# A replanned first phase: seven heads begun on half of D, 2 KB weight rows, K transposed by TensorE, LN statistics split over two engines, all pinned in order

## The chip, the cores and the metric

The kernel runs on one core of a Trainium2 chip. The metric is device time of one execution in microseconds (us), lower is better. All runs named here are of the state "fast"; one core has no second die to compare with.

## The reference

One transformer block with conditioning: a modulation vector from `c`, a layer norm (LN), attention with 32 heads over a cached window of 512 keys in four K/V groups, a second LN, and a SwiGLU block. All arrays are bf16; S = 2048, D = 1024.

```python
mod = (silu(c) @ w_mod).reshape(1, 6, 1, -1)       # sa, ca, ga, sb, cb, gb
h = layernorm(x) * (1 + ca) + sa
q = (h @ wq)                                        # 32 heads of 128
p = softmax(q @ k[last 512].T * 128 ** -0.5)        # k, v from the cache
x = x + ga * ((p @ v) @ wo)
h = layernorm(x) * (1 + cb) + sb
x = x + gb * ((silu(h @ w_gate) * (h @ w_up)) @ w_down)
```

## The kernel before

The sequence is cut into four chunks of 512 rows. After a first phase, which loads x, the columns of `w_mod` and the first weights and makes h of chunk 0, a loop of 128 steps (chunk and head) does attention; the SwiGLU stage follows. In step k TensorE (PE) does the scores of head k, q of a head LEAD steps ahead, side tasks of that step, and the output of head k-1. `at(k, f, ...)` puts a task in step k. All loads and the transposing DMAs go through one queue, that of SyncE (SP). `pin` keeps an instruction in program order on its engine; it is switched off after the loop, and a scheduler orders what isn't pinned.

```python
    for half in range(DH):                 # DMA order of the first phase
        load_wm(1, half)                   # w_mod columns of ca, 1 MB, rows of 1 KB
        load_wm(0, half)                   # of sa
        load_wq(0, 0, (half,))             # wq of heads 0-3, half of D, 0.5 MB
    ...                                    # kT by transposing DMA, then v
    LEAD = 3
    for t in range(QT):                    # LN of chunk 0: four tiles, statistics on DVE
        ln_stats(t)
        n = ln_norm(t, t % 2 == 0)         # tiles 0 and 2 normalised by ACT
        for dt in range(DT):
            nc.tensor.transpose(h0_ps[dt // 4][:, dt % 4, t * P:(t + 1) * P], ...)
        warm(2)                            # dummy matmuls
    for half in range(DH):
        mod_cols(1, half, ca1, True)       # 32 narrow matmuls
        mod_cols(0, half, sa, False)
        ...                                # affine of four dt, then q of heads 0-2 on this half
    # [...]
    at(16 * n + 16, load_cols, n, 2, ..., n == 0)   # small DMA, then 1 + on DVE in the same step
    # [...]
    def plan_late_ln(k, key, sc, sh):      # second LN of the last chunk, in the SwiGLU stage
        for t in range(QT):
            at(k + 2 * t, late_stats, tt)
            at(k + 10 + 2 * t, ln_rows, tt)        # normalise (DVE)
            at(k + 11 + 2 * t, ln_xpose, key, tt)  # transposing DMA
    # [...]
    for k in range(NU + 1):
        if k % 4 >= 2 and 4 * (k // 4) + 8 < NU:
            g = 4 * (k // 4) + 8
            load_wq(g // H, (g % H) // 4, (k % 4 - 2,))   # one half of a wq group
        emit_s(k); emit_q(k + LEAD); run_tasks(k); emit_o(k - 1)   # shortened
    stage.update(dma=False, steps=False)   # from here on nothing is pinned
```

Of the kernel before, what the change touches and what calls it, by code (L numbers as in the profile page):

```python
# [9 lines left out]
ALU = mybir.AluOpType  # L10
# [578 lines left out]
def fast_path(ctx, tc, flag, A_x, A_k_cache, A_v_cache, A_wq, A_wo, B_x, B_w_gate, B_w_up,  # L589
# [36 lines left out]
    k_v = A_k_cache[0][:, k0:k0 + W, :].rearrange("kv (j p) d -> p kv j d", p=P)  # L626
    v_v = A_v_cache[0][:, k0:k0 + W, :].rearrange("kv (j p) d -> p kv j d", p=P)
# [6 lines left out]
    pc_ = ctx.enter_context(tc.tile_pool(name="blkC", bufs=12))  # L634
# [34 lines left out]

    nc.scalar.preload_act_table_set("natural_log_exp_and_others")  # L670
# [23 lines left out]

    for tt in range(QT):
        load_x(tt)
    for half in range(DH):
        load_wm(1, half)
        load_wm(0, half)
        load_wq(0, 0, (half,))  # L700
    kT = blkB("kT", [P, Hkv, W])
    for kv in range(Hkv):
        pin(nc.sync.dma_start_transpose(
            out=kT[:, kv, :], in_=A_k_cache[0, kv, k0:k0 + W, :]), "dma")
# [4 lines left out]
    nc.gpsimd.memset(v_sb[:, :, :, Dh:VN], 1.0)  # L709
    load_wq(0, 1)  # L710


    ident = const.tile([P, P], BF16, name="ident")
    make_identity(nc, ident)
    ones_bf = const.tile([P, P], BF16, name="ones_bf")
# [3 lines left out]

    warm_w = const.tile([P, 512], BF16, name="warm_w")  # L720
    nc.gpsimd.memset(warm_w, 0.5)
    warm_ps = mm("warm_ps")

    def warm(n):
        for _ in range(n):
            tc.keep_in_program_order(
                nc.tensor.matmul(warm_ps, lhsT=ones_bf, rhs=warm_w, start=True, stop=True))

    warm(16)
# [5 lines left out]

    ec = wk.tile([DT, P], FP32, name="ec", tag="f32", bufs=2)
    nc.scalar.activation(out=ec, in_=c_r, func=ACT.Exp, scale=-1.0)
    nc.vector.tensor_scalar(out=ec, in0=ec, scalar1=1.0, scalar2=None, op0=ALU.add)
    rc = wk.tile([DT, P], FP32, name="rc", tag="f32", bufs=2)
    nc.vector.reciprocal(out=rc, in_=ec)  # L740
    sil_r = const.tile([DT, P], BF16, name="sil_r")
    nc.vector.tensor_tensor(out=sil_r, in0=c_r, in1=rc, op=ALU.mult)
    sil_ps = mm("sil_ps", (P, DT), BF16)
    nc.tensor.transpose(sil_ps, sil_r, ident[0:DT, 0:DT])
    siluc = const.tile([P, DT], BF16, name="siluc")
    nc.vector.tensor_copy(out=siluc, in_=sil_ps)
# [11 lines left out]



    sil32 = const.tile([P, DT, 32], BF16, name="sil32")
    for dt in range(DT):
        nc.vector.tensor_scalar(out=sil32[:, dt, :], in0=ones_bf[:, 0:32],
                                scalar1=siluc[:, dt:dt + 1], scalar2=None, op0=ALU.mult)
# [123 lines left out]
    def plan_late_ln(k, key, sc, sh):  # L888

        for t in range(QT):  # L890
            tt = key[1] * QT + t
            at(k + 2 * t, late_stats, tt)
            at(k + 10 + 2 * t, ln_rows, tt)
            at(k + 11 + 2 * t, ln_xpose, key, tt)
        at(k + 8, late_rstd)
        for dt in range(DT):
            at(k + 24 + dt, ln_mod, key, dt, sc, sh)
# [13 lines left out]
    LEAD = 3  # L911
    qT = {}

    def put_q(g, q_ps):
        t = wk.tile([P, TCW], BF16, name="qT", tag="row", bufs=5)
        nc.vector.tensor_copy(out=t, in_=q_ps)  # L916
        qT[g] = t



    new_hT(("h1", 0))
    h0_ps = [big("h0_ps", (P, 4, TCW), BF16) for _ in range(2)]
    for t in range(QT):
        ln_stats(t)
        n = ln_norm(t, t % 2 == 0)
# [3 lines left out]
        warm(2)  # L929
    q0_ps = []  # L930
    for half in range(DH):
        mod_cols(1, half, ca1, True)
        mod_cols(0, half, sa, False)
        for dt in range(4 * half, 4 * half + 4):
            ln_affine(("h1", 0), dt, h0_ps[half][:, dt % 4, :], ca1, sa, dt % 2 == 0)
        if half == 0:
            q0_ps = [mm("q_ps") for _ in range(LEAD)]
        for n in range(4 * LEAD):
            dt, g = (4 * half + n // LEAD, n % LEAD) if half == 0 else (4 + n % 4, n // 4)
            nc.tensor.matmul(q0_ps[g],  # L940
                             lhsT=wq_tiles[(0, 0, dt // 4)][:, dt % 4, g * P:(g + 1) * P],
# [332 lines left out]
```

## Time and profile before

| | before |
|---|---|
| time, median of 4 runs (range) | 1285.27 us (1284.90 to 1288.04) |
| PE busy, share of the span | 1269.7 us, 99% |
| first scores (s_ps) start | 26.46 us |
| PE's longer gaps after that | 0.9 us at 91 us, 2.3 us at 752 us |

The page's head and its first engine line:

```profile
span 1282.7 us, 18139 instructions
...
PE 1269.7 (99%) x7601; PEld 642.9 (50%) x7601; DVE 577.8 (45%) x1271; ACT 333.9 (26%) x433; POOL 1.2 (0%) x8
...
```

PE is the limit everywhere but in the first 30 us. The list of waits from 32 us to the end gives the total, the count and the longest wait in us. A gap quoted in the text runs from the start of one matmul to the start of the next, less their usual spacing (0.216 us for 512 columns); the views count from a modelled end, which makes the same gap about 0.16 us shorter (2.3 us in the table, 2.1 here):

```profile
PE gu_ps L1168 <- DMA wu<-in_B_w_up_dram: 2.1, 1, 2.1
...
PE a_ps L1096 <- DVE acc L1102: 0.7, 1, 0.7
...
```

So what a change can gain lies almost all in the first phase. Its time line (start, duration, engine, instruction, shapes, count; in brackets the idle time before it and what ended it):

```profile
15.62 1.06 PE L927 MATMUL h_ps<-ident,xn 128*128 128x128 bf16 x8
...
17.32 1.51 PE L940 MATMUL q_ps<-hT,wq 128*128 128x512 bf16 x6
...
21.25 0.95 PE L753 MATMUL mod_ps<-siluc,wm 128*128 128x1 bf16 x32 [0.35 <-DMA wm<-in_w_mod_dram]
...
26.46 1.02 PE L1032 MATMUL s_ps<-qT,kT 128*128 128x512 bf16 x4
...
```

The fourth tile's transposes start at 15.6 us, q of the first three heads on the first half of D at 17.3, the last `mod_cols` at 21.25 once the last `wm` has landed, and the scores at 26.46. The windows below give the stretch, its length, the busy us of PE, PEld, DVE, ACT and POOL (instructions in brackets), granted PE clock, DMA share and GB/s:

```profile
12.00:14.00 2.00, 0.85 (x33) 0.86 (x34) 0.00 (x0) 1.38 (x3) 0.00 (x0) 1.00 1.10 348
14.00:16.00 2.00, 2.00 (x18) 1.44 (x16) 0.63 (x2) 0.00 (x0) 0.00 (x0) 0.50 1.10 347
16.00:18.00 2.00, 2.00 (x12) 1.10 (x10) 0.54 (x1) 1.10 (x2) 0.00 (x0) 0.65 1.10 351
...
```

The DMA engines are full at about 350 GB/s, while PE works at a granted clock of 0.50 from 14 to 17.4 us after a thin stretch.

### The profile page before, as it was taken

Reading aid. Unit: us, or ns where it says so; the run is one execution under the profiler, and the core shown is the slowest. Engines: PE = TensorE matmul, PEld = TensorE weight load, DVE = VectorE, ACT = ScalarE, POOL = GpSimd, SP = SyncE. Lnnn points to the kernel's source line nnn. Section 1 sums busy time; section 2 is a strip of 40 time slices with the busy share of each in tenths; the row PEclk is TensorE's granted clock in tenths of the full one; section 3 lists DMA queues with packets and bytes.
Section 4 is the critical chain, followed back from the end, with each engine's and each line's share of the span. In section 5 each row is a group of like instructions: output and inputs, shape, how many; then the busy total and the mean of one; then the engine's idle time right before and its main releaser. Section 6 shows DMA issues by size and latency. Waiting matters only on the chain.

```text
span 1282.7 us, 18139 instructions
## 1 busy us (share of the span) xinstructions
PE 1269.7 (99%) x7601; PEld 642.9 (50%) x7601; DVE 577.8 (45%) x1271; ACT 333.9 (26%) x433; POOL 1.2 (0%) x8
## 2 busy tenths in 40 slices
PE   8999999999999999999999999999999999999998
PEld 4555555555555555555554444444444444444444
DVE  4464467865577755576653642221212221221122
ACT  3543334333333433333341111011100111011100
POOL 0000000000000000000000000000000000000000
PEclk9999999999999999999999999999999999999999
DMA  9888476557355654445487484454536455454401
GB/s 293 269 204 232 152 154 167 141 149 195 91 129 155 144 148 140 123 142 131 132 207 221 142 234 150 140 189 147 181 102 216 143 165 164 135 193 134 146 21 48
DMA packets 280108, 204.21 MB, mean 159 GB/s; under 512 B 113865, under 2 KB 273609, under 8 KB 280018
## 3 DMA queue, kind: packets, MB, share of 16 engines
q1 hardware_dynamic: 275106, 198.78, 54.2%
q10 hardware_dynamic: 4912, 4.20, 1.0%
q8 instruction: 61, 1.00, 0.3%
q14 instruction: 29, 0.24, 0.1%
HBM read 174.08 MB, written 4.21 MB: 139 GB/s over the span
## 4 chain that ended last, share of the span: by engine, by line
PE 95%; DMA 2%; DVE 1%; SPq 1%; ACT 0%; issue 0%; DVEq 0%
PE gu_ps L1168 29%; PE a_ps L1096 17%; PE q_ps L1019 17%; PE d_ps L1188 15%; PE o_ps L1064 9%; PE s_ps L1032 8%; DMA wm<-in_w_mod_dram 1%; SPq L664 1%; DMA hT<-xn 0%; DMA modT<-row_d 0%; DMA wu<-in_B_w_up_dram 0%; PE row_ps L779 0%; PE q_ps L940 0%; DVE st L816 0%; SPq L848 0%; ACT pT L1034 0%
## 5 line engine op out<-in xcount | busy, mean ns | idle before, releaser
L1034 ACT ACTIVATE pT<-s_ps 128x1024 bf16<-128x1024 f32 x256 | 248.7, 1020 | 341.8 <-PE s_ps L1032 341.8
L1096 PE MATMUL a_ps<-wo,oT 128*128 128x512 bf16 x1024 | 241.9, 379 | 0.7 <-DVE acc L1102 0.7
L1019 PE MATMUL q_ps<-hT,wq 128*128 128x512 bf16 x1000 | 236.7, 379 | 0.3 <-DVE modT L755 0.3
L1168 PE MATMUL gu_ps<-hT,wu 128*128 128x512 bf16 x896 | 211.8, 379 | 2.1 <-DMA wu<-in_B_w_up_dram 2.1
L1168 PE MATMUL gu_ps<-hT,wg 128*128 128x512 bf16 x896 | 211.7, 379 | 0.0
L1174 DVE TENSOR_TENSOR guT<-gu_ps,sg 128x512 bf16<-128x512 f32 x112 | 77.4, 691 | 283.5 <-ACT sg L1173 283.5
L1173 ACT ACTIVATE sg<-gu_ps 128x512 bf16<-128x512 f32 x112 | 66.9, 597 | 490.9 <-PE gu_ps L1168 439.7
L1188 PE MATMUL d_ps<-wd,guT 128*128 128x512 bf16 (+2 forms) x952 | 194.2, 366 | 0.0
L916 DVE CAST qT<-q_ps 128x512 bf16<-128x512 f32 x128 | 88.3, 691 | 176.6 <-PE q_ps L1019 176.0
L1096 PEld LDWEIGHTS <-oT 128*128 128x128 bf16 x1024 | 99.9, 98 | 122.1 <-issue 1.9
L1019 PEld LDWEIGHTS <-wq 128*128 128x128 bf16 x1000 | 97.8, 98 | 117.8 <-issue 0.3
L1188 PEld LDWEIGHTS <-guT 128*128 128x128 bf16 x952 | 90.9, 98 | 102.9
L1064 PEld LDWEIGHTS <-pT 128*128 128x128 bf16 x2048 | 126.6, 98 | 30.6 <-issue 0.4
L1168 PEld LDWEIGHTS <-wu 128*128 128x128 bf16 x896 | 87.6, 98 | 108.1 <-DMA wu<-in_B_w_up_dram 2.6
L1168 PEld LDWEIGHTS <-wg 128*128 128x128 bf16 x896 | 87.7, 98 | 105.4
L1064 PE MATMUL o_ps<-v_sb,pT 128*128 128x130 bf16 x2048 | 137.1, 220 | 0.0
L1032 PE MATMUL s_ps<-qT,kT 128*128 128x512 bf16 x512 | 131.5, 379 | 0.6 <-ACT pT L1034 0.6
L1051 DVE TENSOR_TENSOR oq<-o_ps,rl 128x256 bf16<-128x256 f32 (+2 forms) x256 | 101.3, 420 | 4.3
L1192 DVE TENSOR_TENSOR f<-d_ps,gb_bc 128x512 f32<-128x512 f32 (+2 forms) x34 | 22.5, 661 | 147.0 <-PE d_ps L1188 147.0
L1104 DVE TENSOR_TENSOR acc<-a_ps,acc 128x512 f32<-128x512 f32 x64 | 44.1, 689 | 38.9 <-PE a_ps L1096 38.9
L1032 PEld LDWEIGHTS <-kT 128*128 128x128 bf16 x512 | 44.9, 98 | 31.7 <-issue 1.3
L816 DVE BATCH_NORM_STATS2 st<-x 128x6 f32<-128x512 bf16 x64 | 41.3, 680 | 2.9 <-DMA x<-in_A_x_dram 2.6
(75 smaller groups left out, 309.3 us busy)
## 6 DMA issues: line engine op xcount, KB each, us to landing
wq<-in_A_wq_dram SPq DMA_DIRECT2D x64, 512.0 KB, 4.1
wo<-in_A_wo_dram SPq DMA_DIRECT2D x64, 512.0 KB, 5.5
wg<-in_B_w_gate_dram SPq DMA_DIRECT2D x56, 512.0 KB, 5.1
wu<-in_B_w_up_dram SPq DMA_DIRECT2D x56, 512.0 KB, 3.8
wd<-in_B_w_down_dram SPq DMA_DIRECT2D x56, 512.0 KB, 6.4
wmr<-in_w_mod_dram SPq DMA_DIRECT2D x8, 1024.0 KB, 11.4
x<-in_A_x_dram SPq DMA_DIRECT2D x16, 256.0 KB, 5.7
wm<-in_w_mod_dram SPq DMA_DIRECT2D x4, 1024.0 KB, 10.5
```

The costliest lines, as they stand in the source:

```text
L916: nc.vector.tensor_copy(out=t, in_=q_ps)
L1019: nc.tensor.matmul(q_ps, lhsT=wq_tiles[(cc, h // 4, dt // 4)][:, dt % 4, (h % 4) * P:(h % 4 + 1) * P], rhs=hT[("h1", cc)][:, dt, :], start ...
L1032: nc.tensor.matmul(s_ps[:, i, :], lhsT=kT[:, kv, j * P:(j + 1) * P], rhs=qT[g], start=True, stop=True)
L1034: nc.scalar.activation(out=p[:, 2 * jj:2 * jj + 2, :], in_=s_ps, func=ACT.Exp, scale=scale)
L1051: nc.vector.tensor_tensor(out=dst, in0=ps[:, s0:s0 + cnt, 0:Dh], in1=sc, op=ALU.mult)
L1064: nc.tensor.matmul(o_slot["ps"][:, s_, :], lhsT=pT[g][:, j, t * P:(t + 1) * P], rhs=v_sb[:, kv, j, 0:VN], start=(j == 0), stop=(j == WT - 1))
L1096: nc.tensor.matmul(a_ps, lhsT=oT[(cc, 2 * q + i)][:, hh % 4, t * P:(t + 1) * P], rhs=wo_tiles[(cc, q, dh, i)][:, hh % 4, :], start=(hh == ...
L1104: nc.vector.tensor_tensor(out=acc[(cc, t)][:, dsl], in0=a_ps, in1=acc[(cc, t)][:, dsl], op=ALU.add)
L1168: nc.tensor.matmul(ps[:, n, :], lhsT=gu_w[(cc, fg, nm, dt // 4)][:, dt % 4, fi * P:(fi + 1) * P], rhs=hT[("h2", cc)][:, dt, :], start=(dt ...
L1173: nc.scalar.activation(out=g, in_=ps[:, 0, :], func=ACT.Silu)
L1174: nc.vector.tensor_tensor(out=guT[(cc, fg)][:, fi, :], in0=ps[:, 1, :], in1=g, op=ALU.mult)
L1188: nc.tensor.matmul(d_ps, lhsT=guT[(cc, f // 4)][:, f % 4, t * P:(t + 1) * P], rhs=wd_tiles[(cc, dh, f // 4)][:, f % 4, c0:c0 + w], start=( ...
```

## The change

The intent: the phase waits for 5.8 MB (four x tiles of 256 KB, four `wm` of 1024 KB, one wq of 512 KB), so let PE work in that time. Seven heads instead of three are begun on the first half of D. wq comes as rows of 2 KB for eight heads (0.5 MB more before the last `wm`). K is loaded plainly and transposed by PE. Tile 3's statistics go to ACT, the others stay on DVE. The whole phase is chained: every instruction follows the one before it on its engine. Other lines adapt: LN of chunk 1 is planned five steps earlier (LEAD 7 needs it earlier), silu(c) is computed on ACT and GpSimd (POOL) and not on DVE, K's squares (a bound check) move from the last 32 steps to steps 5 to 8, pool C has 11 blocks instead of 12, and the late LN's transposes stand three steps behind their rows. The core of the diff:

```diff
+    H0 = 7
+    def load_wq8(i):                       # rows of 2 KB: eight heads, two dt
+        t = blkB("wq8", [P, 2, 8 * P])
+        load(t, wq_v[:, 2 * i:2 * i + 2, 0:8 * P])
     for half in range(DH):
         load_wm(1, half)
         load_wm(0, half)
-        load_wq(0, 0, (half,))
-    ... pin(nc.sync.dma_start_transpose(out=kT[:, kv, :], ...), "dma")
+        load_wq8(2 * half)
+        load_wq8(2 * half + 1)
+    k_ld = blkA("k_ld", [P, Hkv, WT * Dh])
+    load(k_ld, k_v)
[...]
-    LEAD = 3
+    LEAD = H0
[...]
+    stats_0(0)                             # DVE
+    stats_0(1)
+    xpose_0(0, ln_norm(0))
+    sil_cols()                             # PE transpose of silu(c), then an ACT copy
+    warm(4)
+    stats_act(3)                           # ACT: two passes over tile 3 and five small ones
+    stats_0(2)                             # DVE; its rstd on ACT, behind stats_act(3)
+    xpose_0(1, ln_norm(1))
+    mod_cols(1, 0, ca1, True)
+    xpose_0(2, ln_norm(2))
+    xpose_0(3, ln_norm(3))
[...]
+    q0_big = [big("q_ps") for _ in range(2)]      # heads 0,1 and 2,3 share a tile
+    q0_ps = [q0_big[i // 2][:, i % 2, :] for i in range(4)] + [mm("q_ps") for ...]
[...]
+    for g in range(H0):
+        q0(g, range(4, DT))                # second half of D, head by head
+        put_q(g, q0_ps[g])                 # DVE copies q to SBUF
+        if g == 4:
+            k_xpose(0)
+    chain(first)
[...]
-            at(k + 10 + 2 * t, ln_rows, tt)       # late LN
-            at(k + 11 + 2 * t, ln_xpose, key, tt)
+            at(k + 10 + 4 * t, ln_rows, tt)
+            at(k + 13 + 4 * t, ln_xpose, key, tt)
[...]
+    for kv in range(1, Hkv):
+        at(kv, k_xpose, kv)
-        at(NU - H + 20 + 2 * kv, bound_k, kv)
+        at(5 + kv, bound_k, kv)
-        plan_ln((cc - 1) * H + (10 if cc == 1 else 2), ("h1", cc), ca1, sa)
+        plan_ln((cc - 1) * H + (5 if cc == 1 else 2), ("h1", cc), ca1, sa)
```

More of the change, by code (lines that the diff above doesn't have):

```diff
@@ L625, in fast_path @@
     c_v = c.rearrange("o (dt p) -> (o dt) p", p=P)
-    k_v = A_k_cache[0][:, k0:k0 + W, :].rearrange("kv (j p) d -> p kv j d", p=P)
-    v_v = A_v_cache[0][:, k0:k0 + W, :].rearrange("kv (j p) d -> p kv j d", p=P)
+    k_v = A_k_cache[0][:, k0:k0 + W, :].rearrange("kv (p j) d -> p kv (j d)", j=WT)
+    v_v = A_v_cache[0][:, k0:k0 + W, :].rearrange("kv (p j) d -> p kv j d", j=WT)
     const = ctx.enter_context(tc.tile_pool(name="const", bufs=1))
@@ L633, in fast_path @@
     pb_ = ctx.enter_context(tc.tile_pool(name="blkB", bufs=7))
-    pc_ = ctx.enter_context(tc.tile_pool(name="blkC", bufs=12))
+    pc_ = ctx.enter_context(tc.tile_pool(name="blkC", bufs=11))
     wk = ctx.enter_context(tc.tile_pool(name="work", bufs=2))
@@ L668, in load, with chain @@
             fetch(out=out, in_=in_)
+    def chain(start):
+        last = {}
+        for ins in nc.cur_bb.bb.instructions[start:]:
+            if ins.engine in last:
+                tc.add_manual_dep(
+                    ins, last[ins.engine],
+                    mybir.DependencyInfo(mybir.DependencyClass.NoSync,
+                                         mybir.DependencyReason.DATA), reason="chain")
+            last[ins.engine] = ins.name
+    first = len(nc.cur_bb.bb.instructions)
     nc.scalar.preload_act_table_set("natural_log_exp_and_others")
@@ L693, in load_wq @@
             wq_tiles[(cc, hg, i)] = t
+    H0 = 7
+    wq8 = []
+    def load_wq8(i):
+        t = blkB("wq8", [P, 2, 8 * P])
+        load(t, wq_v[:, 2 * i:2 * i + 2, 0:8 * P])
+        wq8.append(t)
     for tt in range(QT):
@@ L699, in fast_path @@
         load_wm(0, half)
-        load_wq(0, 0, (half,))
-    kT = blkB("kT", [P, Hkv, W])
-    for kv in range(Hkv):
-        pin(nc.sync.dma_start_transpose(
-            out=kT[:, kv, :], in_=A_k_cache[0, kv, k0:k0 + W, :]), "dma")
+        load_wq8(2 * half)
+        load_wq8(2 * half + 1)
+    k_ld = blkA("k_ld", [P, Hkv, WT * Dh])
+    load(k_ld, k_v)
     VN = Dh + 2
@@ L708, in fast_path @@
         load(v_sb[:, kv, :, 0:Dh], v_v[:, kv])
-    nc.gpsimd.memset(v_sb[:, :, :, Dh:VN], 1.0)
-    load_wq(0, 1)
+    load_wq(0, 2)
     ident = const.tile([P, P], BF16, name="ident")
     make_identity(nc, ident)
+    warm_w = const.tile([P, 512], BF16, name="warm_w")
+    nc.gpsimd.memset(warm_w, 0.5)
     ones_bf = const.tile([P, P], BF16, name="ones_bf")
@@ L718, in fast_path @@
     nc.vector.memset(eps_t, eps)
-    warm_w = const.tile([P, 512], BF16, name="warm_w")
-    nc.gpsimd.memset(warm_w, 0.5)
     warm_ps = mm("warm_ps")
@@ L725, in warm @@
         for _ in range(n):
-            tc.keep_in_program_order(
-                nc.tensor.matmul(warm_ps, lhsT=ones_bf, rhs=warm_w, start=True, stop=True))
-    warm(16)
+            nc.tensor.matmul(warm_ps, lhsT=ones_bf, rhs=warm_w, start=True, stop=True)
     modT = const.tile([P, 4, DT], FP32, name="modT")
@@ L733, in fast_path, with sil_cols @@
     gb_bc = const.tile([P, D], FP32, name="gb_bc")
+    warm(18)
     ec = wk.tile([DT, P], FP32, name="ec", tag="f32", bufs=2)
     nc.scalar.activation(out=ec, in_=c_r, func=ACT.Exp, scale=-1.0)
-    nc.vector.tensor_scalar(out=ec, in0=ec, scalar1=1.0, scalar2=None, op0=ALU.add)
-    rc = wk.tile([DT, P], FP32, name="rc", tag="f32", bufs=2)
-    nc.vector.reciprocal(out=rc, in_=ec)
+    nc.scalar.activation(out=ec, in_=ec, func=ACT.Ln, bias=1.0)
+    nc.scalar.activation(out=ec, in_=ec, func=ACT.Exp, scale=-1.0)
     sil_r = const.tile([DT, P], BF16, name="sil_r")
-    nc.vector.tensor_tensor(out=sil_r, in0=c_r, in1=rc, op=ALU.mult)
-    sil_ps = mm("sil_ps", (P, DT), BF16)
-    nc.tensor.transpose(sil_ps, sil_r, ident[0:DT, 0:DT])
+    nc.gpsimd.tensor_tensor(out=sil_r, in0=c_r, in1=ec, op=ALU.mult)
+    nc.gpsimd.memset(v_sb[:, :, :, Dh:VN], 1.0)
     siluc = const.tile([P, DT], BF16, name="siluc")
-    nc.vector.tensor_copy(out=siluc, in_=sil_ps)
+    sil32 = const.tile([P, DT, 32], BF16, name="sil32")
+    def sil_cols():
+        sil_ps = mm("sil_ps", (P, DT), BF16)
+        nc.tensor.transpose(sil_ps, sil_r, ident[0:DT, 0:DT])
+        nc.scalar.copy(out=siluc, in_=sil_ps)
+        for dt in range(DT):
+            nc.gpsimd.tensor_scalar(out=sil32[:, dt, :], in0=ones_bf[:, 0:32],
+                                    scalar1=siluc[:, dt:dt + 1], scalar2=None, op0=ALU.mult)
     def mod_cols(vec, half, dst, add_one):
@@ L756, in mod_cols @@
                                 scalar1=1.0 if add_one else 0.0, scalar2=None, op0=ALU.add)
-    sil32 = const.tile([P, DT, 32], BF16, name="sil32")
-    for dt in range(DT):
-        nc.vector.tensor_scalar(out=sil32[:, dt, :], in0=ones_bf[:, 0:32],
-                                scalar1=siluc[:, dt:dt + 1], scalar2=None, op0=ALU.mult)
     wm_rows = []
@@ L892, in plan_late_ln @@
             at(k + 2 * t, late_stats, tt)
-            at(k + 10 + 2 * t, ln_rows, tt)
-            at(k + 11 + 2 * t, ln_xpose, key, tt)
+            at(k + 10 + 4 * t, ln_rows, tt)
+            at(k + 13 + 4 * t, ln_xpose, key, tt)
         at(k + 8, late_rstd)
         for dt in range(DT):
-            at(k + 24 + dt, ln_mod, key, dt, sc, sh)
+            at(k + 28 + dt, ln_mod, key, dt, sc, sh)
     def plan_ln(k, key, sc, sh):
@@ L908, in plan_ln, with xpose_0 @@
             at(k + 11 + dt, ln_mod, key, dt, sc, sh)
-    LEAD = 3
+    LEAD = H0
     qT = {}
     def put_q(g, q_ps):
-        t = wk.tile([P, TCW], BF16, name="qT", tag="row", bufs=5)
+        t = wk.tile([P, TCW], BF16, name="qT", tag="row", bufs=LEAD + 2)
         nc.vector.tensor_copy(out=t, in_=q_ps)
         qT[g] = t
-    new_hT(("h1", 0))
     h0_ps = [big("h0_ps", (P, 4, TCW), BF16) for _ in range(2)]
-    for t in range(QT):
-        ln_stats(t)
-        n = ln_norm(t, t % 2 == 0)
+    def xpose_0(t, n):
         for dt in range(DT):
@@ L928, in fast_path @@
                                 n[:, dt * P:(dt + 1) * P], ident)
-        warm(2)
-    q0_ps = []
-    for half in range(DH):
-        mod_cols(1, half, ca1, True)
-        mod_cols(0, half, sa, False)
-        for dt in range(4 * half, 4 * half + 4):
-            ln_affine(("h1", 0), dt, h0_ps[half][:, dt % 4, :], ca1, sa, dt % 2 == 0)
-        if half == 0:
-            q0_ps = [mm("q_ps") for _ in range(LEAD)]
-        for n in range(4 * LEAD):
-            dt, g = (4 * half + n // LEAD, n % LEAD) if half == 0 else (4 + n % 4, n // 4)
-            nc.tensor.matmul(q0_ps[g],
-                             lhsT=wq_tiles[(0, 0, dt // 4)][:, dt % 4, g * P:(g + 1) * P],
-                             rhs=hT[("h1", 0)][:, dt, :], start=(dt == 0), stop=(dt == DT - 1))
@@ L943, in fast_path, with rstd_0, stats_0, stats_act @@
-    for g in range(LEAD):
+    def rstd_0(t):
+        mv = ln[t]
+        nc.scalar.activation(out=mv[:, 2:3], in_=mv[:, 1:2], func=ACT.Ln, bias=eps_t)
+        nc.scalar.activation(out=mv[:, 2:3], in_=mv[:, 2:3], func=ACT.Exp, scale=-0.5)
+    def stats_0(t):
+        mv = ln[t] = sm.tile([P, 4], FP32, name="mv", tag="mv", bufs=4)
+        ln_stats(t, mv)
+        rstd_0(t)
+    def stats_act(t):
+        mv = ln[t] = sm.tile([P, 4], FP32, name="mv", tag="mv", bufs=4)
+        junk = wk.tile([P, D], BF16, name="junk", tag="junk", bufs=1)
+        nc.scalar.activation(out=junk, in_=xt[t], func=ACT.Identity, accum_out=mv[:, 3:4])
+        nc.scalar.activation(out=mv[:, 0:1], in_=mv[:, 3:4], func=ACT.Identity, scale=1.0 / D)
+        nc.scalar.activation(out=mv[:, 3:4], in_=mv[:, 3:4], func=ACT.Identity, scale=-1.0 / D)
+        junk = wk.tile([P, D], BF16, name="junk", tag="junk", bufs=1)
+        nc.scalar.activation(out=junk, in_=xt[t], func=ACT.Square, bias=mv[:, 3:4],
+                             accum_out=mv[:, 1:2])
+        nc.scalar.activation(out=mv[:, 1:2], in_=mv[:, 1:2], func=ACT.Identity, scale=1.0 / D)
+        rstd_0(t)
@@ new lines, in fast_path @@
+    stats_0(0)
[9 more added lines that the diff above has]
+    xpose_0(3, ln_norm(3))
+    new_hT(("h1", 0))
+    h10 = hT[("h1", 0)]
+    nc.scalar.copy(out=h10[:, 4:8, :], in_=h0_ps[1])
+    nc.vector.tensor_copy(out=h10[:, 0:2, :], in_=h0_ps[0][:, 0:2, :])
+    nc.vector.tensor_copy(out=h10[:, 2:4, :], in_=h0_ps[0][:, 2:4, :])
+    warm(4)
+    mod_cols(0, 0, sa, False)
@@ new lines, in fast_path, with affine_0, w0, q0 @@
+    warm(2)
+    def affine_0(half):
+        for dt in range(4 * half, 4 * half + 4):
+            ln_mod(("h1", 0), dt, ca1, sa)
+    def w0(g, dt):
+        return wq8[dt // 2][:, dt % 2, g * P:(g + 1) * P]
+    affine_0(0)
+    q0_big = [big("q_ps") for _ in range(2)]
+    q0_ps = [q0_big[i // 2][:, i % 2, :] for i in range(4)] + [mm("q_ps") for _ in range(H0 - 4)]
+    def q0(g, dts):
+        for dt in dts:
+            nc.tensor.matmul(q0_ps[g], lhsT=w0(g, dt), rhs=h10[:, dt, :], start=(dt == 0),
+                             stop=(dt == DT - 1))
@@ new lines, in fast_path, with k_xpose @@
+    for dt in range(4):
+        for g in range(H0):
+            q0(g, (dt,))
+        if dt == 2:
+            mod_cols(1, 1, ca1, True)
+    mod_cols(0, 1, sa, False)
+    affine_0(1)
+    kT = blkB("kT", [P, Hkv, W])
+    def k_xpose(kv):
+        ps = mm("k_ps", (P, WT, P), BF16)
+        for j in range(WT):
+            nc.tensor.transpose(ps[:, j, :], k_ld[:, kv, j * Dh:(j + 1) * Dh], ident)
+        nc.scalar.copy(out=kT[:, kv, :], in_=ps.rearrange("p j k -> p (j k)"))
+    for g in range(H0):
+        q0(g, range(4, DT))
@@ L944, in fast_path @@
         put_q(g, q0_ps[g])
-    k_ld = []
+        if g == 4:
+            k_xpose(0)
+    chain(first)
     NSQ = 2 * 2 * (H // 4)
@@ L956, in bound_wq @@
                                            op1=ALU.mult, accum_out=sq[:, col:col + 1]))
-    def load_k():
-        k_ld.append(blkA("k_ld", [P, Hkv, WT, Dh]))
-        for kv in range(Hkv):
-            load(k_ld[0][:, kv], k_v[:, kv])
     kk = const.tile([P, Hkv * WT], FP32, name="kk")
@@ L968, in bound_k @@
             junk = wk.tile([P, Dh], BF16, name="junk", tag="junk", bufs=1)
-            src = k_ld[0][:, kv, j, :]
+            src = k_ld[:, kv, j * Dh:(j + 1) * Dh]
             pin(nc.vector.scalar_tensor_tensor(out=junk, in0=src, scalar=1.0, in1=src,
@@ L1018, in emit_q @@
         for dt in range(DT):
-            nc.tensor.matmul(q_ps,
-                             lhsT=wq_tiles[(cc, h // 4, dt // 4)][:, dt % 4,
-                                                                 (h % 4) * P:(h % 4 + 1) * P],
+            w = w0(g, dt) if g < 8 else wq_tiles[(cc, h // 4, dt // 4)][:, dt % 4, (h % 4) * P:
+                                                                        (h % 4 + 1) * P]
+            nc.tensor.matmul(q_ps, lhsT=w,
                              rhs=hT[("h1", cc)][:, dt, :], start=(dt == 0), stop=(dt == DT - 1))
@@ L1128, in fast_path @@
                 at((1 + hg % (NTC - 1)) * H + max(0, 4 * hg - 3 + 2 * i + j), bound_wq, hg, i, j)
-    at(NU - H + 2, load_k)
+    for kv in range(1, Hkv):
+        at(kv, k_xpose, kv)
     for kv in range(Hkv):
-        at(NU - H + 20 + 2 * kv, bound_k, kv)
-    at(NU - H + 29, bound_mod)
+        at(5 + kv, bound_k, kv)
+    at(10, bound_mod)
     at(NU + 3, bound_final)
@@ L1171, in emit_gu @@
                                  stop=(dt == DT - 1))
-        g = wk.tile([P, TCW], BF16, name="sg", tag="row", bufs=5)
+        g = wk.tile([P, TCW], BF16, name="sg", tag="row", bufs=LEAD + 2)
         nc.scalar.activation(out=g, in_=ps[:, 0, :], func=ACT.Silu)
@@ L1192, in emit_down @@
             nc.vector.tensor_tensor(out=r, in0=d_ps, in1=gb_bc[:, dsl], op=ALU.mult)
-            o = wk.tile([P, w], BF16, name="o_sb", tag="row", bufs=5)
+            o = wk.tile([P, w], BF16, name="o_sb", tag="row", bufs=LEAD + 2)
             nc.vector.tensor_tensor(out=o, in0=r, in1=xt[cc * QT + t][:, dsl], op=ALU.add)
@@ L1203, in fast_path @@
     for k in range(NU + 1):
-        if k % 4 >= 2 and 4 * (k // 4) + 8 < NU:
-            g = 4 * (k // 4) + 8
+        if k % 4 >= 2 and 4 * (k // 4) + 12 < NU:
+            g = 4 * (k // 4) + 12
             load_wq(g // H, (g % H) // 4, (k % 4 - 2,))
@@ L1210, in fast_path @@
             emit_q(k + LEAD)
-        if k == NU - 4:
+        if k == NU - 5:
             load_gu(0, 0)
```

## The prediction

> **What bounds it.** The page's busy table gives PE 1269.7 of 1282.7 us. The list of waits shows that after 32 us PE waited only about 2.8 us in all (2.1 of it at 752 to 755 us for a `wu` load). The window table shows the loss in the first phase. At 32.31 us, when s_ps of the third head starts, PE has done five q heads, two score heads, one output head: 48 matmuls of 512 columns (10.36 us at the 0.216 us spacing of the steady stretches) and 16 narrow ones (0.91), 11.3 us. So the start costs 21.0 us. That is all that a better first phase could win, so 2% (25.7 us) is out of reach.
>
> **Why 21 us before.** DMA: from 8 to 20 us the 16 engines are full at 348 GB/s (1 KB rows). The chain waits for `wm` until 21.2 us; then 5 us of halved heads, then PE waits for the first exps.
>
> **What the change does.**
> 1. DMA: 2 KB rows (windows with 2 KB loads move 377 to 406 GB/s), but 0.5 MB more before the last `wm`, 1.05 MB more before q can end. Estimate from these rates: last `wm` lands at 22.0, last wq8 at 24.7 us (21.2 and about 22 before).
> 2. Seven heads rather than three, 28 matmuls on each half of D (6.05 us each): PE waits less for the second half, and the first exps are covered.
> 3. A new serial chain, pinned. warm(18), transposes of tile 0 (about 9 us), the siluc copy, and only then ACT's statistics of tile 3: passes of 128x1024 at 1.0 to 1.24 us twice, six small ones of 0.2 to 0.3: about 13.7 us, because tile 2's rstd stands behind it. Normalisations (0.53 each) and transposes end at about 16.4 us, cold: PE idles from about 11.7 to 14.3. The Trainium skill ("TensorE: Matmul & The Clock Gate", Part 1) says that idling about 3.4 us halves the clock; the trace agrees that a thin stretch does: granted clock 0.50 from 14 to 16 us. Then PSUM copies (2 x 1.0 us DVE, 1.9 us ACT), warm(4), mod_cols, affine: q starts at about 19.8 us, after its data.
> 4. From there PE is bound by itself: 12.1 us of q, 1.9 of mod_cols, about 0.8 of affine wait, 0.3 of K transposes: done at about 35.0 us. That is 22.9 us lost; 12 more K transposes (0.07 us) 0.8: 23.7 against 21.0, so **+2.7 us**.
> 5. K's squares now fall in steps 5 to 8 beside LN statistics: 16 x 0.37 us of DVE; DVE lags up to 3 us, the PSUM slots bear about that: **+0.3**.
> 6. Late LN: transposes now three steps after their rows, so the SP queue no longer stands before `wu`: **-2.1**, and LEAD 7 and earlier weights perhaps -0.3.
> 7. One C block fewer: no PE wait expected.
>
> Sum +0.6; I lean 0.7 back for the chance that ACT's statistics or the cold clock are milder: **1285.0 us**, 8 in 10 within 1280.5 to 1289.0. Faster by over 2%: 0.01; same 0.98; slower 0.01.
>
> **What would show it.** After: first q matmul of the first phase at 19 to 21 us, not at 15 to 16; PE idle 11.7 to 14.3 us for xn; last wq8 landed before PE wants it; first s_ps at 34 to 36 us; no wait for `wu` at 750 us; K transposes on ACT and PE at steps 0 to 3.
>
> **What would make it wrong.** If the statistics end by 12 us, q starts with its data at 15 to 16 us, PE ends at about 31 us, and the kernel gains 3 to 4 us. If PE stays cold through q's first half, or C blocks or DVE's backlog hold PE, it loses up to 4 us more.

## The result and the profile after

| | before | after |
|---|---|---|
| time, median of 4 runs (range) | 1285.27 us (1284.90 to 1288.04) | 1291.93 us (1290.45 to 1293.36) |
| ratio of fast runs, 95% interval | | 1.0047 (1.0029 to 1.0065) |
| span of the profiled run | 1282.7 us | 1291.6 us |
| first q matmul | 17.3 us | 19.05 us |
| first scores start | 26.46 us, three q heads and six of the fourth's eight matmuls done | 36.08 us, seven done |

A ratio is the mean time of one kernel's fast runs over that of the other's of the same rounds, so not quite the ratio of the medians quoted. The kernel before was run anew on each chip; its medians there are 1285.3 to 1287.3 us. The change is slower by about half a per cent, inside the 2% band but outside the range that I had stated. The profiled run is the slowest of the four, and a part of it (below) is not in every run.

```profile
span 1291.6 us, 18173 instructions
...
PE 1273.1 (99%) x7621; PEld 644.6 (50%) x7621; DVE 577.0 (45%) x1262; ACT 336.5 (26%) x442; POOL 4.3 (0%) x17
...
```

PE's waits after 40 us, all that exceed 1 us; the first two answer to the two shown of before, the third is new:

```profile
PE gu_ps L1236 <- DMA wu<-in_B_w_up_dram: 2.3, 1, 2.3
PE a_ps L1163 <- DVE acc L1169: 2.2, 1, 2.2
...
PE q_ps L1088 <- DMA wq<-in_A_wq_dram: 1.7, 1, 1.7
...
```

The time line of the first phase after:

```profile
9.35 0.17 ACT L762 COPY siluc<-sil_ps 128x8 bf16<-128x8 bf16 x1 [2.44 <-PE sil_ps L761]
9.42 1.06 ACT L951 ACTIVATE junk<-x 128x1024 bf16<-128x1024 bf16 x1
...
11.07 1.15 ACT L955 ACTIVATE junk<-x,mv 128x1024 bf16<-128x1024 bf16 x1
...
13.56 1.00 DVE L847 TENSOR_SCALAR xn<-x,mv 128x1024 bf16<-128x1024 bf16 x2 [1.84 <-ACT mv L941]
...
14.16 1.57 PE L935 MATMUL h_ps<-ident,xn 128*128 128x128 bf16 x16 [2.65 <-DVE xn L847]
...
19.05 4.69 PE L993 MATMUL q_ps<-hT,wq 128*128 128x512 bf16 x21 [0.34 <-DVE hT L868]
...
28.99 0.69 DVE L928 CAST qT<-q_ps 128x512 bf16<-128x512 f32 x1 [0.20 <-PE q_ps L993]
29.73 1.89 PE L993 MATMUL q_ps<-hT,wq 128*128 128x512 bf16 x8 [0.78 <-DVE qT L928]
...
36.08 1.03 PE L1099 MATMUL s_ps<-qT,kT 128*128 128x512 bf16 x4
...
```

ACT starts tile 3's statistics only behind the copy of `siluc` (9.35 us). Tile 2's rstd (one over its standard deviation) stands behind them, so DVE can normalise tiles 2 and 3 only from 13.56 us; PE transposes them from 14.16 us, having waited 2.65. From there to the first q matmul at 19.05 us come PSUM copies, four dummies at half clock, `mod_cols` and the affine (LN's scale and shift). In the second half of D, PE stands 0.94 us between the last matmul of head 0 and the first of head 1 (0.78 of them in the bracket at 29.73), waiting for the copy at 28.99, and again before 32.40 us. The windows to set against those of before:

```profile
12.00:14.00 2.00, 0.00 (x0) 0.00 (x0) 0.44 (x1) 1.40 (x7) 0.32 (x1) 1.00 1.06 376
14.00:16.00 2.00, 1.84 (x18) 1.56 (x19) 1.22 (x4) 0.24 (x1) 0.00 (x0) 0.64 1.09 368
16.00:18.00 2.00, 2.00 (x32) 1.16 (x31) 0.63 (x2) 1.63 (x1) 0.00 (x0) 0.51 1.10 347
...
```

PE did nothing from 12 to 14 us, and its clock was at half from 14.55 to 17.96.

After the first phase the chain of waits (start, duration, what) shows two more losses:

```profile
79.12 1.65 SPq L1148
...
80.81 5.10 DMA wq<-in_A_wq_dram
...
85.96 1.04 PE q_ps L1088 x4
...
99.30 5.48 DMA modT<-row_d
...
104.80 0.07 DVE modT L814
...
105.33 0.61 DVE acc L1169
...
105.98 2.90 PE a_ps L1163 x8
...
```

At 80.81 us a wq load was issued that PE wanted at 84. At 99.30 a small load of `modT` was issued; DVE, which adds 1 to it in the same step, stood until it landed; PE waited 2.23 us for DVE's copy of the a_ps before (L1169), which stood behind that addition, and then ran eight matmuls in 2.90 us, not 1.89: the clock record has 0.50 from 106.7 to 110.1 us.

To add this up, I set the start of each step's o_ps matmuls in one trace against the same step in the other. The difference is 10.69 us from head 2 to head 11. Of these 6.91 are four more q heads done (32 matmuls of 0.216), which come back at the end of the loop when q is missing. The rest is loss:

| where | us |
|---|---|
| first phase, with the K transposes of steps 1 to 3 | 3.78 |
| wait for wq, ahead of o_ps of head 12 | 1.86 |
| wait behind `modT`, ahead of o_ps of head 15: gap of 2.40, against 0.89 before | 1.51 |
| half clock after that gap, heads 15 and 16 | 1.66 |
| wait for `wu` in the SwiGLU stage: 2.44 against 2.26 | 0.18 |
| sum, which is the difference of the last matmuls | 8.99 |

The timed runs differ by 6.7 us (medians); the half clock, as the experiments show, does not come in every run.

The late LN, from which I expected a gain, looks as before. SP's queue at that point, before and after:

```profile
743.56 6.84 SPq L848 DMA_TRANSPOSE hT<-xn  x4
750.50 0.53 SPq L664 DMA_DIRECT2D wu<-in_B_w_up_dram  x1
...
```

```profile
752.38 6.98 SPq L860 DMA_TRANSPOSE hT<-xn  x4
759.45 0.53 SPq L664 DMA_DIRECT2D wu<-in_B_w_up_dram  x1
...
```

In both the four transposes of hT were issued in one block of almost 7 us, and the load of `wu` that PE waited for stood behind it. The three steps of distance which the change writes are not in the instruction stream: the stage is not pinned.

### The profile page after: what moved, and what is told of

Its sections match the earlier page's. It is cut to its first block, busy times and chain, and to the rows that moved or that the text cites. A ratio compares the mean times of both kernels' runs of the same rounds, so it can differ in the third digit from the quotient of the medians.

```text
span 1291.6 us, 18173 instructions
## 1 busy us (share of the span) xinstructions
PE 1273.1 (99%) x7621; PEld 644.6 (50%) x7621; DVE 577.0 (45%) x1262; ACT 336.5 (26%) x442; POOL 4.3 (0%) x17
## 4 chain that ended last, share of the span: by engine, by line
PE 96%; DMA 2%; DVE 1%; ACT 0%; SPq 0%; issue 0%; POOL 0%; POOLq 0%; DVEq 0%
PE gu_ps L1236 29%; PE a_ps L1163 17%; PE q_ps L1088 16%; PE d_ps L1256 15%; PE o_ps L1131 9%; PE s_ps L1099 8%; PE q_ps L993 1%; PE warm_ps L741 1%; DMA modT<-row_d 0%; DMA wq<-in_A_wq_dram 0%; DMA hT<-xn 0%; DMA wu<-in_B_w_up_dram 0%; PE row_ps L791 0%; PE mod_ps L772 0%; DVE qT L928 0%
## 5 line engine op out<-in xcount | busy, mean ns | idle before, releaser
L1088 PE MATMUL q_ps<-hT,wq 128*128 128x512 bf16 x968 | 228.8, 379 | 1.7 <-DMA wq<-in_A_wq_dram 1.7
L1088 PEld LDWEIGHTS <-wq 128*128 128x128 bf16 x968 | 94.6, 98 | 116.2 <-DMA wq<-in_A_wq_dram 2.2
L1260 DVE TENSOR_TENSOR f<-d_ps,gb_bc 128x512 f32<-128x512 f32 (+2 forms) x34 | 22.4, 660 | 147.1 <-PE d_ps L1256 147.1
```

The costliest lines, as they stand in the source:

```text
L1088: nc.tensor.matmul(q_ps, lhsT=w, rhs=hT[("h1", cc)][:, dt, :], start=(dt == 0), stop=(dt == DT - 1))
```

## The experiments

Twelve kernels ran, all correct. The table has the timed results; the text below then goes through them.

| run | what | median us (range) | ratio to before, 95% |
|---|---|---|---|
| changed kernel | | 1291.93 (1290.45 to 1293.36) | 1.0047 (1.0029 to 1.0065) |
| e1_dve_stats | changed, tile 3's statistics on DVE | 1289.45 (1288.88 to 1291.90) | 1.0029 (1.0016 to 1.0042) |
| e2_head_order | changed, other order of the seven heads | 1288.64 (1287.01 to 1289.62) | 1.0013 (0.9999 to 1.0027) |
| e3_late_add | changed, 1 + done eight steps later | 1288.77 (1288.13 to 1290.78) | 1.0017 (1.0004 to 1.0031) |
| e4_wq_first | changed, wq ahead of the transposes | 1287.56 (1287.38 to 1291.28) | 1.0012 (0.9998 to 1.0025) |
| e8_bound_k_later | changed, K's squares in steps 18 to 21 | 1289.39 (1287.92 to 1290.17) | 1.0022 (1.0009 to 1.0035) |
| e7_before_c11 | before, 11 blocks in pool C | 1286.19 (1284.39 to 1290.05) | 1.0000 (0.9985 to 1.0015) |
| e5_all_four | e1 to e4 together | 1282.40 (1282.10 to 1282.79) | 0.9969 (0.9956 to 0.9982) |
| e10_all_pin | e5 and the second stage pinned | 1282.18 (1281.53 to 1285.17) | 0.9967 (0.9954 to 0.9980) |
| e14_all_pin_bk | e10 and K's squares later | 1280.92 (1279.15 to 1282.20) | 0.9956 (0.9941 to 0.9972) |
| e15_all_pin_bk_warm | e14 and six dummies | 1280.39 (1279.34 to 1282.35) | 0.9957 (0.9941 to 0.9973) |
| e12_before_late_pin | before, late 1 + and pinning | 1296.18 (1292.54 to 1296.93) | 1.0063 (1.0045 to 1.0081) |
| e16_before_repaired | e12 with the change's late LN spacing | 1282.14 (1281.76 to 1284.18) | 0.9960 (0.9947 to 0.9974) |

The changed kernel itself was not run again beside these. Against its median the single edits gained 2.48 us (e1), 3.29 (e2), 3.16 (e3), 4.37 (e4) and 2.54 (e8). The first four add up to 13.3 us, while e5, which holds all four, gained 9.5. So the medians bear out the sum of the traces (8.9 us) for the four together, and what one edit is worth is read from the traces. The other parts of the new first phase (rows of 2 KB, K transposed by PE, silu(c) on ACT and GpSimd, the chaining) were not undone one by one; what they cost or gain lies in the 3.78 us of the first phase and is not shown.

### e1_dve_stats: the split of the statistics

```diff
-    stats_act(3)
     stats_0(2)
     xpose_0(1, ln_norm(1))
+    stats_0(3)
```

> The changed kernel with the statistics of tile 3 back on DVE (placed after tile 2's), one part of the change undone. My theory: tile 2's rstd no longer stands behind two ACT passes, so the transposes end at about 13.4 us instead of 15.7, the first q matmul of the first phase starts at 16.5 to 17 us instead of 19.05, the first s_ps at about 33.7 us instead of 36.08, and the kernel gains 2 to 3 us on the changed one (1291.9 to about 1289.5); the waits at steps 12 and 15 stay. Rival (the first phase is bound by the 1.05 MB more of weights): q starts earlier but waits for wq8 or wm, first s_ps stays at about 36, no gain.

Measured: the first q matmul starts at 15.51 us and the first scores at 33.43 instead of 36.08. PE's time line, cut at 18 us:

```profile
11.99 1.08 PE L935 MATMUL h_ps<-ident,xn 128*128 128x128 bf16 x16 [0.74 <-DVE xn L847]
...
15.51 2.75 PE L993 MATMUL q_ps<-hT,wq 128*128 128x512 bf16 x12 [0.34 <-DVE hT L868]
```

The 16 transposes of tiles 2 and 3 start at 11.99 instead of 14.16 us and no half clock stands in the records before the end. q begins 3.5 us earlier; 2.65 of them arrive at the scores, because PE now waits for data in between (gaps of 0.62 and 0.46 us). So the split was a loss of 2.65 us, half clock included (that this equals the wait of 2.65 us at 14.16 is chance): ACT spent 3.1 us (9.42 to 12.54) on what DVE does for another tile in 1.5 (1.28 for the two statistics instructions and 0.21 for the aggregate), and with tile 3's own rstd (until 13.10) it stood in front of tile 2's rstd. The figure is good to about 0.7 us: the same first phase, not edited, reached the scores at 36.08, 35.36, 35.71 and 36.02 us in the profiles of the changed kernel, e3, e4 and e8. The rival, a phase bound by its additional bytes, is refuted as the cause of the lateness, but the new gaps show that this limit lies close behind.

### e2_head_order: two heads in one PSUM tile

```diff
-    for g in range(H0):
+    for g in (0, 2, 4, 1, 3, 5, 6):
         q0(g, range(4, DT))
         put_q(g, q0_ps[g])
-        if g == 4:
+        if g == 5:
```

> The changed kernel with the seven heads finished in the order 0, 2, 4, 1, 3, 5, 6 instead of 0 to 6, so that no two heads which share a PSUM tile follow each other. My theory: the two gaps of 0.94 us between q matmuls (at 28.6 and 31.2 us), in which PE waits for DVE's copy of the head before, vanish: first s_ps at about 34.2 us instead of 36.08, gain 1.7 to 1.9 us (1291.9 to about 1290.1). Rival (PE waits there for DVE's speed or for data, whatever the tile): the gaps stay or move.

Measured: the gaps are gone, 23 matmuls run in one piece, and the scores start at 34.12 us, 1.95 earlier:

```profile
27.54 5.66 PE L993 MATMUL q_ps<-hT,wq 128*128 128x512 bf16 x23 [0.78 <-DVE hT L868]
...
34.12 1.03 PE L1099 MATMUL s_ps<-qT,kT 128*128 128x512 bf16 x4
...
```

So PE waited because head 1 goes into the tile which DVE still read for head 0. (PSUM is the memory that takes the results of matmuls.) The Trainium skill ("PSUM — Partial Sum Buffer", Terms) gives a bank as 2 KiB per partition, and each head's half of the tile (512 fp32 elements) is just that; the two halves need not share a bank, yet the wait was there. It follows the tile, as the new order shows; who in the tool chain makes it so was not looked into.

### e3_late_add: DVE's stand behind a small load

```diff
-        at(16 * n + 16, load_cols, n, 2, sb if n else cb1, n == 0)
+        at(16 * n + 16, load_cols, n, 2, sb if n else cb1, False)
+        if n == 0:
+            at(24, add_cols, cb1)          # the 1 +, pinned
```

> The changed kernel with the 1 + of the second LN's scale taken out of step 16 and done in step 24, so that DVE does not stand 5.5 us for the landing of that small load. My theory: the gap of 2.4 us before a_ps at 103 us goes, and with it the 3.4 us at a granted clock of 0.50 that follow it (1.7 us): gain 3.5 to 4.1 us (1291.9 to about 1288). If the clock drop is not a consequence of that gap, gain only 2.4 us and a 0.50 stretch remains in the records of the clock. Rival (PE waits there for DVE's backlog from K's squares and LN): the gap shrinks but stays.

Measured: no gap over 0.25 us stands at 100 to 106 us. The half clock there is gone as well, but one of 3.4 us appears at 760.5 us, behind the `wu` gap (2.31 us). In e2 and e4 the gap at 101 us was still there, 2.47 us each, and no half clock followed. So the gap is DVE's wait for its own load, as I thought; the half clock follows such a gap in some profiles and not in others. Counting the fourteen gaps of 1.96 to 2.64 us after 60 us in the profiles of before, after, e1 to e5, e7 and e8, four were followed by a stretch of 3.4 us at 0.50. The Trainium skill ("TensorE: Matmul & The Clock Gate", Part 1) describes a free-running window of 3413 ns; the records agree with stretches of 3.41, 6.83 or (in e10) 10.24 us, and a window whose start doesn't follow the kernel would explain why the same gap is sometimes punished. It was not tested by itself.

### e4_wq_first: the order of the SP queue

```diff
-        if k % 4 >= 2 and 4 * (k // 4) + 12 < NU:
+        if k % 4 == 2 and 4 * (k // 4) + 12 < NU:
             g = 4 * (k // 4) + 12
-            load_wq(g // H, (g % H) // 4, (k % 4 - 2,))
+            load_wq(g // H, (g % H) // 4)
```

> The changed kernel with both halves of each wq group issued ahead of the four transposes of oT in the SP queue, in steps 4m+2, instead of one half behind them. My theory: the wait of 1.85 us for wq at 84 us is that queue's order (the load was issued at 80.8 us, after 7.3 us of transposes): it vanishes, gain 1.9 us or a little more (1291.9 to about 1290). Rival (the DMA engines are short of bandwidth there, or the one block fewer in C holds the queue): the wait stays.

Measured: the wait for wq is gone (1.86 us at head 12 in the traces). The four transposes now take 8.7 us of the queue, behind both loads, and PE doesn't wait for it:

```profile
71.95 1.08 SPq L664 DMA_DIRECT2D wq<-in_A_wq_dram  x2
...
73.63 8.72 SPq L1148 DMA_TRANSPOSE oT<-oq  x4
...
```

Neither bandwidth nor blocks were short. The Trainium skill ("DMA: Bandwidth & Descriptors", Anatomy of one DMA — SWDGE (gpsimd) path) says of DMA engines in general that a semaphore wait happens on the issuing sequencer before dispatch; the trace of the changed kernel agrees for SP's queue: the wq load behind the transposes, which ended at 80.76 us, was issued at 80.81.

### e8_bound_k_later: K's squares, and a theory that fell

```diff
-        at(5 + kv, bound_k, kv)
-    at(10, bound_mod)
+        at(18 + kv, bound_k, kv)
+    at(23, bound_mod)
```

> The changed kernel with the squares of K in steps 18 to 21 and not 5 to 8. My prediction gave these DVE instructions 0.3 us of PE time, by DVE's backlog. My theory now: they cost PE nothing in steps 5 to 8, no gap larger than 0.25 us stands there in the trace, and moving them changes neither the wait at 84 us by more than 0.5 us nor the time by more than 1 us (1291.9). Rival (DVE's backlog delays oq, and with it the transposes that stand ahead of the wq load): the gap at 84 us shrinks by over 1 us.

My theory fell, by the wait and by the time (2.5 us, not under 1): the wait of 1.85 us at 84 us is gone here too, with the queue's order unchanged. SP's queue in the changed kernel and then in this run:

```profile
73.44 7.32 SPq L1148 DMA_TRANSPOSE oT<-oq  x4
80.81 0.58 SPq L664 DMA_DIRECT2D wq<-in_A_wq_dram  x1
...
```

```profile
72.11 6.80 SPq L1148 DMA_TRANSPOSE oT<-oq  x4
78.96 0.58 SPq L664 DMA_DIRECT2D wq<-in_A_wq_dram  x1
...
```

The block of transposes is 0.5 us shorter, began 1.3 us sooner and ended 1.8 us sooner, so the load behind it was issued at 78.96 instead of 80.81 us and landed in time. The 16 squares delayed DVE's rows and output copies (the transpose of hT ahead of this block stands at 68.80 and not at 70.41 us); the transposes wait for those; the wq load waits for the transposes. So DVE's backlog did cost PE 1.86 us, by way of the SP queue and not of PSUM slots. Order and backlog are links of one chain, and cutting either was enough.

### e7_before_c11: one block fewer

```diff
-    pc_ = ctx.enter_context(tc.tile_pool(name="blkC", bufs=12))
+    pc_ = ctx.enter_context(tc.tile_pool(name="blkC", bufs=11))
```

> The kernel before with 11 blocks in pool C instead of 12, that part of the change alone. My theory: no PE wait comes of it, within 0.5 us of the kernel before (ratio 0.9995 to 1.0005). Rival (the missing block holds the SP queue and is behind the waits at 84 and 103 us): slower by 1 to 5 us.

Measured: ratio 1.0000 (0.9985 to 1.0015). The interval is wider than the band that I had named, but 1 to 5 us slower is excluded beyond 2 us. The gap before a_ps was 1.64 us in its profile (0.89 in that of before), so a part of the 1.5 us in the sum above may be chance as well, or come of the block. In the changed kernels that keep this gap it was 1.64 (e1), 1.98 (e8), 2.40 and 2.47 us (e2, e4).

### e5_all_four and e10_all_pin: do the parts add?

e5 is the sum of the four edits above. e10 adds:

```diff
-    stage.update(dma=False, steps=False)
+    stage.update(dma=True, steps=True)
```

> The changed kernel with all four edits of the earlier experiments at once (tile 3's statistics on DVE, head order 0 2 4 1 3 5 6, the late 1 +, wq ahead of the transposes). My theory: the four costs are separate and on PE's path, so they add: in the traces 2.65, 1.95, 2.4 and 1.86 us, 8.9 together, so 1291.9 becomes about 1283, a little below the kernel before (1285.8 in the last batch): ratio 0.997 to 0.999. If a limit that they share (DMA in the first phase) lies close behind, the sum falls short and it stays at 1285 to 1287.

> The same with the queue and step order kept in program order in the second stage too, so that the late transposes of h2 stay three steps behind their rows, as the plan has them, instead of being hoisted in a block of four ahead of a wu load. My theory: the gap of 2.0 to 2.5 us between gu matmuls at about 755 us, which both kernels have, is that block in the SP queue; it goes, 1.5 to 2.5 us faster than the run with four edits (about 1281). Rival: the pinned order puts wd loads ahead of gate and up weights and makes new gaps at the starts of the chunks; then it is equal or slower.

e5 landed where the sum of the traces put it: 1282.40 us, a ratio of 0.9969, and the scores start at 30.98 us. Now DMA shows as the next limit; the waits from 15 to 31 us contain

```profile
PEld L994 <- DMA wq<-in_A_wq_dram: 1.4, 2, 0.9
...
PE mod_ps L772 <- DMA wm<-in_w_mod_dram: 0.2, 1, 0.2
```

e10 lost the `wu` gap, as its trace shows. Its transposes of hT stand singly, behind the weight loads:

```profile
765.88 11.59 SPq L664 DMA_DIRECT2D wu<-in_B_w_up_dram  x2
778.05 1.28 SPq L861 DMA_TRANSPOSE hT<-xn  x1
...
```

From the last o_ps to the last matmul it took 601.0 us and e5 603.3. The medians don't show these 2.3 us: in e10's profiled run PE's clock was at half from 11.75 to 21.99 us, its scores started at 35.1 us, and its runs spread by 3.6 us. So the gain of the pinning is shown in the stage and not in the total of this pair.

### e12_before_late_pin and e16_before_repaired: what the new first phase is worth

e12 is the kernel before with the late 1 + and the pinning. e16 is e12 with the change's spacing of the late LN (rows at k + 10 + 4t, transposes at k + 13 + 4t, affine from k + 28).

> The kernel before, its first phase untouched, with two of the repairs alone: the late 1 + and the pinned order of the second stage. My theory: the two waits that it shares with the changed kernel (0.9 us before a_ps at 91 us, 2.3 us before gu at 752 us) go, 3 us faster than the kernel before (ratio about 0.9977). Compared with the run of four edits and pinning (ratio 0.9967) this says what the new first phase is worth when it is repaired: about 1 to 1.5 us. If the new phase were worth the 5 us that seven heads begun early suggest, the distance would be larger.

> The kernel before with its old first phase, and with the late 1 +, the pinned second stage and the late LN's rows and transposes three steps apart as in the change. My theory after the failed run with the pinning alone: pinned order is good only together with the wider spacing; the new gaps of 4.2 and 3.8 us at 778 and 799 us go, the gaps at 91 and 752 us stay away, and the time is about 3 us below the kernel before (ratio 0.9970 to 0.9985). Against the best version (ratio 0.9956) that leaves 2 to 3 us for the repaired new first phase. Rival (pinning hurts this kernel whatever the spacing): gaps stay, slower than before.

e12 went wrong: the gap at 91 us is gone, but pinned with the old spacing the queue stands at each transpose, and PE waited 4.2 us at 778 us and 3.8 us at 799:

```profile
776.63 1.28 SPq L849 DMA_TRANSPOSE hT<-xn  x1
778.00 1.10 SPq L664 DMA_DIRECT2D wg<-in_B_w_gate_dram  x2
...
792.75 6.25 SPq L849 DMA_TRANSPOSE hT<-xn  x2
799.06 1.15 SPq L664 DMA_DIRECT2D wd<-in_B_w_down_dram  x2
```

With the wider spacing (e16) those are gone, and there is no gap over 0.5 us after 32 us. The ratio is 0.9960 (0.9947 to 0.9974), better than I expected. The trace gives what I expected: from o_ps of head 2 to the last matmul e16 takes 3.10 us less than the kernel before; its first phase was 2.88 us longer in that profile, so this trace doesn't explain the rest of the ratio. So distance and pinning are one measure: distance alone did nothing in the changed kernel, pinning alone cost some 8 us by the ratio in the kernel before (with half clock after both gaps in its record), both together removed the wait. The comparison that I wanted is e16 with e14: 0.9960 against 0.9956, the old first phase against the repaired new one. The new one's advantage is not to be told from zero with intervals of 0.0015 on either side. The traces place it. From o_ps of head 2 on e14 gains 3.15 us on the kernel before (four q heads taken off), e16 3.10, so only the first phase differs. Measured at that o_ps, and against the kernel before, the old first phase came 0 (before), 0.80 (e7), 1.40 (e12) and 2.88 us (e16) late, each with 3.4 to 6.8 us of half clock in it; the repaired new one came 1.32 (e5), 1.91 (e15) and 2.25 us (e14) early without half clock, and 2.82 late (e10) with 10.2 us of it. What it is worth hangs on the clock, and these few profiles don't settle it.

### e14_all_pin_bk and e15_all_pin_bk_warm

e14 is e10 with the edit of e8. e15 adds `warm(3)` before and after the first `mod_cols`.

> The four edits and the pinned second stage, and K's squares in steps 18 to 21 besides. My theory: with wq issued ahead of the transposes the squares no longer reach PE, so this equals the run with four edits and pinning (about 1282): the two cures of the wait at 84 us are cures of one chain and do not add. Rival: DVE's backlog costs PE something else in steps 5 to 8; then 0.5 to 1 us faster.

> The same with three dummy matmuls before and three after the first mod_cols, so that PE has no thin stretch from 8 to 13 us. My theory: the spread of 3 to 4 us among runs of one kernel comes of the granted clock in the first phase (in one profile it stood at 0.50 from 11.7 to 21.9 us and cost about 4 us); with PE fed, no 0.50 stretch stands in the first 25 us and the runs lie within 1 us of each other, at 1281 to 1282.5. Rival (the spread has other causes): runs still spread by 3 us, median unchanged or 0.5 us worse for the dummies.

e14 is the best version with e15: 1280.9 us, faster than the kernel before by 0.4% and than the changed one by 0.9% (that one by medians from two chips), less than 2% both. It doesn't differ from e10 beyond the intervals. The traces are sharper: from o_ps of head 2 to the last matmul e10, e14 and e15 agree within 0.02 us, so with wq ahead of the transposes the squares cost nothing more, and the two cures are cures of one chain.

e15's runs still spread by 3.0 us, so the forecast of 1 us failed. But the theory behind it is not refuted. The profiled runs of e14 and e15, which show no half clock before the end, are the fastest of their runs (1279.15 and 1279.34 us), and e10's, with 10.2 us of it in the first phase, is its slowest (1285.17 us); the 4.7 to 5.1 us between their traces all lie ahead of o_ps of head 2. Every timed run also has a mean granted clock on record. In e15 the three runs at 0.999 took 1279.34 to 1280.39 us and the two at 0.998 took 1281.94 and 1282.35; in e12 the run at 0.997 took 1292.54 and the two at 0.991 took 1296.18 and 1296.93. In e2 no such order shows. So the spread goes with the clock in most batches; where in the slower runs of e15 the clock fell is not on record, and what decides it stays open.

## Why the prediction was wrong

I expected 1285.0 us (1280.5 to 1289.0) and measured 1291.93. From the sum of the prediction (+0.6 before the lean) to the 8.99 us of the profiled pair:

- **Bound and ceiling: right.** PE bound throughout, 21 us lost at the start, so no 2%.
- **Step 1, DMA: right where it can be seen.** In e5 PE waits for the last `wm` up to 22.4 us and for wq8 up to 25.1; I had 22.0 and 24.7. In the changed kernel all data came before PE asked.
- **Step 3, the serial chain: right.** ACT done at 13.7 forecast, 13.5 measured; PE idle 11.7 to 14.3, measured 11.5 to 14.15; half clock from 14.5; first q at 19.8 forecast, 19.05 measured. e1 confirms the cause.
- **Step 4, "done at about 35.0 us", +2.7: right mechanism, one term missing.** 36.08 and +3.78 measured. The missing term is the two waits of 0.94 us between heads that share a PSUM tile (e2: 1.95 us); q's start, 0.75 us sooner than forecast, hid a part of it. I had counted the matmuls and not who still reads the tile they write to.
- **Step 5, "the PSUM slots bear about that: +0.3": wrong.** The backlog that I computed was real, but the first to suffer was not PSUM. It delayed the transposes in the SP queue and with them a wq load: 1.86 us (e4, e8).
- **Step 6, "the SP queue no longer stands before `wu`: -2.1", and -0.3: wrong.** Measured +0.18. I read the plan of steps as if it were the order of instructions. Without pinning the four transposes were issued as one block again. This is the largest error among the terms of the sum, 2.6 us. That it was the order of issue is shown by e10 and e16, where pinning removed the wait.
- **Not in the sum:** DVE's stand for `modT`. I had seen the 0.7 us it cost before and did not ask what it would be after the shift; it was 2.4 (excess 1.5), and 1.7 more by half clock in the profiled run. With the 1.1 us of step 4 and the 1.6 and 2.6 of steps 5 and 6 this accounts for the distance from +0.6 to 8.99.
- **Step 7, one C block fewer: not contradicted.** e7 excludes a cost beyond 2 us and can't tell a smaller one.
- **The lean of 0.7 us** towards a gain had no number behind it.

In short: the effects in the first phase were worked out one by one and came out near; those on the far side of a shared queue or of a small load were judged by the plan's text, and there the sum was 2.6 + 1.6 + 1.5 us too low.

## What to carry to other kernels

A distance written into a plan exists only if something holds it in the instruction stream: compare the issue order of the queue, not the source. When work moves to an idle engine, look at what stands behind it in that engine's order; here 3.7 us of statistics and rstd on idle ACT delayed another tile's rstd, and PE stood 2.65 us for it. In a queue shared by loads and waiting transposes, a few us of backlog on a slack engine reach the busiest one through the next load behind them.

## What the Trainium skill lacked or had wrong

- "TensorE: Matmul & The Clock Gate" (Part 1 and its practical rules) names single gaps of about 3 to 3.4 us as those to avoid. Here gaps of 2.3 to 2.6 us were followed by 3.4 us at a granted clock of 0.50 in four of fourteen cases (counted from 1.96 us on), which cost 1.66 us in the one that was measured.
- The same page gives no measure of how thin the work may get before the clock falls. In the kernel before, 32 `mod_cols` matmuls of one column with a wait of 1.5 us before them, and no idle gap of 3 us, were followed by 0.50 from 14.0 to 17.4 us.
- "DMA: Bandwidth & Descriptors" gives sequencer times of transposing DMAs for small tiles from HBM and for 8,192 tiles in SBUF, none for a transpose of 128x512 or 128x1024 bf16 in SBUF: it held the queue for 1.23 to 1.31 us each here where it did not have to wait, and a block of four for 5.1 us and more, during which no load of that queue was issued.
- The two ScalarE pages tell of the accumulator output but not of what it adds to a pass; here the passes over 128x1024 bf16 took 1.06 and 1.15 us, and a separate instruction of 0.19 us read the accumulator.
